# Windowed attention and a mixer block on one core: q and k tails transposed together, small scores moved, PSUM banks in turn

## The chip, the cores and the metric

The kernel runs on one core of a Trainium2 chip. The metric is the time of one execution on the device in microseconds (us). One execution was also recorded by the hardware profiler; times of single instructions come from that record. TensorE (PE, with its weight loads PEld) multiplies matrices into PSUM, which has eight banks here; VectorE (DVE) and ScalarE (ACT) read PSUM; GpSimd (POOL) works in SBUF; SyncE (SP) issues most DMAs. Each engine works through its own queue in order.

## What is computed

For each of 8 batches, attention over 8 heads with a window, and then a mixer block:

```python
scores = q @ k.T / 8                     # 8 batches, 8 heads, 576 positions, 64 wide
mask   = (0 <= i - j < 32)                           # heads 0 to 3
mask   = (0 <= i - j < 128) and (i - j) % 4 == 0     # heads 4 to 7
attn   = softmax(where(mask, scores, -1e9)) @ v
x      = attn with its heads side by side            # 8 x 576 x 512
u      = x + (relu(x.T @ w_tok1) @ w_tok2).T         # 576 -> 256 -> 576
out    = u + relu(u @ w_ch1) @ w_ch2                 # 512 -> 1536 -> 512
```

Inputs and outputs are fp32; the kernel computes in fp16 with fp32 sums in PSUM.

## The kernel before, in words

**Work of one batch.** POOL casts q, k and v to fp16 (names c_q, c_k, c_t, vv, vt). c_t holds the last 64 positions ("the tail") of q in its partitions 0 to 63 and of k in 64 to 127. For each pair of heads (hp 0 to 3; 0 and 1 have the plain window, 2 and 3 the dilated one), `transposes` (line 254) is called once for q and once for k. Each call makes four 128x128 transposes on TensorE (line 262) and a fifth of the tail (lines 266, 268), all into one bank, tp_q or tp_k. The tail transpose covers q's and k's tails together each time, and a permutation (`perm`) brings the wanted half to where it is read. The bank is then copied to SBUF: k by VectorE into kt (line 270), q into qz in two copies of 64 partitions, by ScalarE for pairs 0 and 1 (line 95) and by VectorE for pairs 2 and 3 (line 97).

The scores of a pair come in three steps (`scores_plain`, `scores_dil`, both with the product in line 284): the first scores of either head, each in one bank sc, and the "small scores" of both heads in a bank sm, which need the last keys. ScalarE takes the exponentials (lines 304, 313, 316 and 333, 341) and POOL multiplies them with the mask (line 107; batch 0 and part of batch 1 add the mask on TensorE, line 283). `values` multiplies with v into av, and VectorE divides (rec, xn). `emit_h1`, `emit_u` and `emit_uT` are the token mixer: h1p, up and tpu in PSUM, h1, u and uT in SBUF. `gen_main` is the channel mixer: 24 groups gp of four matmuls (line 496), each evicted by relu into gt (ACT line 101, DVE line 103), then groups yp (line 513; the two tails of an odd batch in line 533), summed with u into o (lines 523, 537) and stored.

**Order.** Batch 0 is prepared in an order written out by hand (calls `tp`, `sc`, `va`, `mx`). Then iteration b runs the channel mixer of batch b, and between its groups the steps of later batches: values and token mixer of batch b+1, transposes and scores of batch b+2 (iteration 0 does the scores of batches 1 and 2). `score_steps`, `value_steps` and `mix_steps` give each step a due time and a cost, and `interleave` calls a step when the sum of the costs so far reaches its due time. Nothing reorders afterwards: that is each engine's queue.

**PSUM.** `bank` (line 90) hands out banks under three tags: "fl" with three (tp_q, tp_k, av, h1p, up, tpu), "main" with three (gp, yp) and "sc" with two (sc, and sm from batch 1 on). Which of a tag's banks a tile gets is left to the pool. A matmul that starts a new tile in a bank waits until the copies out of the tile before have ended.

Of the kernel before, what the change touches and what calls it, by code (L numbers as in the profile page):

```python
# [16 lines left out]
S = 576  # L17
# [11 lines left out]
MR = S // 4  # L29

RS = 160
BLK = 160
# [6 lines left out]
GW = 2 * S  # L39


def _np_perm(first):

    m = np.zeros((128, 128), dtype=np.float16)
    for r in range(4):
        for i in range(32):
            half = (i // 16 + first) % 2
            m[64 * half + 4 * (i % 16) + r, 32 * r + i] = 1.0
    return m


def _np_band():
    p = np.arange(128)[:, None]
    rel = np.arange(BLK)[None, :] - p
    return ((rel >= 0) & (rel < WINDOW)).astype(np.float16)
# [14 lines left out]
def kernel(  # L70
# [11 lines left out]
    nc = tc.nc  # L82
# [4 lines left out]
    def fixed(name, shape, dtype=FP16):  # L87
        return sb.tile(shape, dtype, tag=name, bufs=1, name=name)

    def bank(tag, bufs, name, dtype=FP32):  # L90
        return ps.tile([128, 512 if dtype == FP32 else 1024], dtype, tag=tag, bufs=bufs, name=name)

    def copy(eng, out, in_):
        if eng is nc.scalar:
            nc.scalar.copy(out=out, in_=in_)  # L95
        else:
            eng.tensor_copy(out=out, in_=in_)  # L97
# [7 lines left out]
    def mult(eng, out, a, b):  # L105
# [1 line left out]
        eng.tensor_tensor(out=out, in0=x, in1=y, op=ALU.mult)  # L107


    CW = 3 * 128 + BLK + 128  # L110
    const = fixed("const", [128, CW])
    ident = const[:, 0:128]
    perm = [const[:, 128:256], const[:, 256:384]]
    band = const[:, 384:384 + BLK].rearrange("p (x y c) -> p x y c", x=1, y=1)
    dtail = const[:, 384 + BLK:CW].rearrange("p (x y c) -> p x y c", x=1, y=2)

    veil = fixed("veil", [128, BLK + 128])

    spread = fixed("spread", [128, 515])
    const_np = np.concatenate(  # L120
        [np.eye(128, dtype=np.float16), _np_perm(0), _np_perm(1), _np_band(),
         _np_dtail().reshape(128, 128)], axis=1)
    const_dram = nc.inline_tensor(const_np, name="consts").ap()

    qz = [fixed(f"qz{i}", [128, 2, S]) for i in range(4)]
    kt = [fixed(f"kt{i}", [128, 640]) for i in range(4)]
# [83 lines left out]
    c16 = {}  # L210
# [40 lines left out]
    def natural(ap):  # L251
        return ap.rearrange("p (m r) -> p m r", r=4)

    def transposes(b, nm, hp):
        c = c16[(b, nm)]
        p = bank("fl", 3, f"tp_{nm}_{b}_{hp}", FP16)
        tail = c16[(b, "t")][:, 2 * hp:2 * hp + 2, :].rearrange("m h d -> m (h d)")
        grid = p[:, 0:4 * RS].rearrange("p (r i) -> p r i", i=RS)
        got = grid[:, :, 0:MR].rearrange("p r m -> p m r")
        flat = nm == "q" and hp >= 2  # L260
        for r in range(4):
            nc.tensor.transpose(  # L262
                out=p[:, 128 * r:128 * r + 128] if flat else grid[:, r, 0:128],
                in_=c[:, r, 2 * hp:2 * hp + 2, :].rearrange("m h d -> m (h d)"), identity=ident)
        if flat:
            nc.tensor.transpose(out=p[:, 512:640], in_=tail, identity=ident)  # L266
        else:
            nc.tensor.transpose(out=grid[:, :, 128:RS], in_=tail, identity=perm[nm == "k"])  # L268
        if nm == "k":
            nc.vector.tensor_copy(out=natural(kt[hp][:, 0:S]), in_=got)  # L270
            return
        eng = nc.vector if hp >= 2 else nc.scalar
        for h in range(2):
            rows = slice(64 * h, 64 * h + 64)
            if flat:
                copy(eng, qz[hp][rows, h], p[rows, 0:S])
            else:
                copy(eng, natural(qz[hp][rows, h]), got[rows])

    def score(b, hp, h, out, keys, queries, hide):  # L280

# [144 lines left out]
    def emit_uT(b, cb):  # L426
        odd = b % 2
        c = slice(128 * cb, 128 * cb + 128)
        p = bank("fl", 3, f"tpu_{b}_{cb}", FP16)
        tl = u16t[b // 2][:, c]  # L430
        t = sb.tile([128, S], FP16, tag="ut", bufs=5, name=f"uT_{b}_{cb}")
        eng = nc.scalar if cb >= 2 else nc.vector
        if cb < 2:
            m0, t0, c0 = (128, 0, 64) if odd else (0, 512, 0)
            for s in range(4):
                nc.tensor.transpose(out=p[:, m0 + 128 * s:m0 + 128 * s + 128],
                                    in_=u16[(b, s)][:, c], identity=ident)
            nc.tensor.transpose(out=p[:, t0:t0 + 128], in_=tl, identity=ident)
            copy(eng, t, p[:, c0:c0 + S])
        else:  # L440
            grid = p[:, 0:4 * RS].rearrange("p (r i) -> p r i", i=RS)
            m0, t0, c0 = (32, 0, 16) if odd else (0, 128, 0)
            for s in range(4):
                nc.tensor.transpose(out=grid[:, s, m0:m0 + 128], in_=u16[(b, s)][:, c], identity=ident)  # L444
            nc.tensor.transpose(out=grid[:, :, t0:t0 + 32], in_=tl, identity=perm[0])  # L445
            copy(eng, natural(t), grid[:, :, c0:c0 + MR].rearrange("p r m -> p m r"))
        uT[(b, cb)] = t


    def score_steps(b, t0, dt):  # L450
        steps = []
        for hp in range(4):
            at = t0 + hp * dt
            for nm in ("q", "k"):
                steps.append((at + 0.9 * (nm == "k"), 0.28, lambda nm=nm, hp=hp: transposes(b, nm, hp)))
            g = (scores_plain if hp < 2 else scores_dil)(b, hp)
            for i in range(3):
                steps.append((at + dt + 0.6 * i, 0.21, lambda g=g: next(g)))
        return steps

    def value_steps(b, t0, dt):
# [6 lines left out]
            steps.append((t0 + dt * h, 0.29 if h < 4 else 0.18, step))  # L468
        return steps

    def mix_steps(b, t_h1, t_h1b, t_u, t_uT):
        if b % 2 == 0 and b // 2 not in u16t:
            u16t[b // 2] = sb.tile([128, DM], FP16, tag="u16t", bufs=2, name=f"u16t_{b // 2}")
        h1 = [sb.tile([128, DM], FP16, tag="h1", bufs=4, name=f"h1_{b}_{jb}") for jb in range(2)]
        steps = []
        for half, at in ((0, t_h1), (1, t_h1b)):
            for jb in range(2):
                steps.append((at + 0.9 * jb, 0.55, lambda jb=jb, half=half: emit_h1(b, jb, half, h1[jb])))
        for i, s in enumerate((4, 0, 1, 2, 3)):
            steps.append((t_u + 1.0 * i, 0.44, lambda s=s: emit_u(b, s, h1)))  # L480
        for i, cb in enumerate(CBS):
            steps.append((t_uT + 0.9 * i, 0.28, lambda cb=cb: emit_uT(b, cb)))
        return steps
# [99 lines left out]
    def gate(t, src):  # L583
# [1 line left out]

    cast_qk(0, "q", 0, nc.scalar)
    cast_qk(0, "k", 0, nc.vector)
    nc.vector.tensor_scalar(out=veil, in0=const[:, 384:CW], scalar1=1.0, scalar2=60000.0,
                            op0=ALU.subtract, op1=ALU.mult)
    cast_tails_qk(0, nc.vector)  # L590
    cast_qk(0, "q", 1, nc.gpsimd)
# [21 lines left out]
    for jb in range(2):  # L613
        nc.gpsimd.tensor_copy(
            out=w2p[jb], in_=w2[jb][:, 0:512].rearrange("p (m r) -> p r m", r=4))
# [56 lines left out]
    for i, n in enumerate(((0, 2), (2, 4), (4, 5))):  # L672
        nc.gpsimd.dma_start(
            out=w4a[:, 4 * i:4 * i + 4],
            in_=moe_w_ch2[512 * i:512 * i + 512, :].rearrange("(p i) c -> p i c", i=4))
# [13 lines left out]
    def at(t0, dt, fs):  # L689
        return [(t0 + dt * i, 0.0, f) for i, f in enumerate(fs)]  # L690
# [5 lines left out]
    for b in range(B):  # L696
        steps = []
        if b == 0:
            first, dil = score_steps(1, 5.5, 2.6), score_steps(1, 12.0, 2.0)
            steps += first[:10] + dil[10:]  # L700
            steps += at(14.4, 0.3, casts1_dil) + at(16.0, 0.5, casts1[9:])
            steps += at(15.7, 0.0, [lambda nm=nm: load_qk(2, nm, 4, 8, nc.sync) for nm in ("q", "k")])
            steps += at(23.0, 0.0, [lambda: load_v(2)])
            casts = cast_steps(2)
            steps += value_steps(1, 20.2, 0.7)
            steps += mix_steps(1, 23.0, 26.6, 28.2, 32.9) + score_steps(2, 25.4, 2.1)
            steps += at(21.7, 0.5, casts[:9]) + at(32.5, 0.3, casts[9:])
            steps += at(36.0, 0.0, [lambda: emit_loads_qk(3)])
        elif b == 1:
            steps += value_steps(2, 4.2, 1.0) + mix_steps(2, 10.0, 14.0, 16.6, 21.6)  # L710
            steps += score_steps(3, 21.0, 2.8) + at(8.0, 0.6, cast_steps(3))
            steps += at(6.0, 0.0, [lambda: load_v(3)]) + at(20.0, 3.0, [lambda: emit_loads_qk(4), lambda: load_v(4)])
        else:
            if b + 1 < B:
                steps += value_steps(b + 1, 0.6, 1.1) + mix_steps(b + 1, 6.6, 10.6, 13.2, 18.2)
            if b + 2 < B:
                steps += at(2.0, 0.6, cast_steps(b + 2)) + score_steps(b + 2, 20.6, 2.8)
            if b + 3 < B:
                steps += at(13.0, 3.0, [lambda b=b: emit_loads_qk(b + 3), lambda b=b: load_v(b + 3)])
        interleave(gen_main(b), steps)  # L720
# [30 lines left out]
```

## Time and profile before

| what | value |
|---|---|
| time, median of 3 runs | 320.54 us (320.04 to 321.05) |
| the profiled execution's own time | 320.02 us |
| its span, first to last instruction | 318.1 us |
| TensorE busy | 303.6 us, 3311 matmuls |
| VectorE, ScalarE, POOL busy | 166.2, 154.0, 152.9 us |
| granted TensorE clock | 1.0 throughout |
| DMA | 43.27 MB, mean 136 GB/s |
| the largest two groups, gp (line 496) and yp (line 513) | 109.4 and 91.9 us busy |

A row of the groups gives line, engine, operation, out<-in, shapes and count, then busy time in us and mean ns of one, then the engine's idle time ahead of them and what ended it. A row of the timeline gives the start in us from the span's start, the duration, the engine and line, and in brackets the idle time before it. Matmuls overlap, and their ends are modelled. The iterations of the channel mixer begin at about 31.1, 76.6, 114.5, 150, 187.5, 222.5, 260 and 289.6 us.

### The profile page before, as it was taken

Reading aid. Unit: us, or ns where it says so; the run is one execution under the profiler, and the core shown is the slowest. Engines: PE = TensorE matmul, PEld = TensorE weight load, DVE = VectorE, ACT = ScalarE, POOL = GpSimd, SP = SyncE. Lnnn points to the kernel's source line nnn. Section 1 sums busy time; section 2 is a strip of 40 time slices with the busy share of each in tenths; the row PEclk is TensorE's granted clock in tenths of the full one; section 3 lists DMA queues with packets and bytes.
Section 4 is the critical chain, followed back from the end, with each engine's and each line's share of the span. In section 5 each row is a group of like instructions: output and inputs, shape, how many; then the busy total and the mean of one; then the engine's idle time right before and its main releaser. Section 6 shows DMA issues by size and latency. Waiting matters only on the chain.

```text
span 318.1 us, 8187 instructions
## 1 busy us (share of the span) xinstructions
PE 303.6 (95%) x3311; PEld 269.2 (85%) x3311; DVE 166.2 (52%) x356; ACT 154.0 (48%) x349; POOL 152.9 (48%) x218
## 2 busy tenths in 40 slices
PE   6888999989999999999999999999999999999995
PEld 2676888869978889899987999899987999899884
DVE  6564536773736545555745636545745636532221
ACT  2674594385445535365554635465454725413500
POOL 8771466569840896019930797009940670000000
PEclk9999999999999999999999999999999999999999
DMA  8999999823945979711593139811000220012022
GB/s 214 276 195 244 193 243 277 242 77 84 339 110 154 273 226 285 158 43 58 149 290 89 40 107 297 163 36 68 33 2 5 63 101 3 0 48 86 2 68 99
DMA packets 66597, 43.27 MB, mean 136 GB/s; under 512 B 35936, under 2 KB 64992, under 8 KB 66560
## 3 DMA queue, kind: packets, MB, share of 16 engines
q1 hardware_dynamic: 63328, 37.63, 43.2%
q0 software_dynamic: 1632, 3.94, 6.7%
q10 hardware_dynamic: 1600, 1.18, 1.4%
q8 instruction: 26, 0.43, 0.6%
q14 instruction: 11, 0.09, 0.1%
HBM read 37.07 MB, written 9.44 MB: 146 GB/s over the span
## 4 chain that ended last, share of the span: by engine, by line
PE 87%; DVE 5%; ACT 5%; issue 1%; POOL 0%; ACTq 0%; POOLq 0%
PE gp L496 29%; PE yp L513 25%; PE up L407 4%; PE h1p L395 4%; PE sc L284 4%; PE yp L533 3%; PE tp_q L262 2%; PE sm L284 2%; PE idle_p L561 2%; ACT qz L95 2%; PE tp_k L262 1%; PE h1p L393 1%; DVE kt L270 1%; PE tpu L444 1%; PE av L371 1%
## 5 line engine op out<-in xcount | busy, mean ns | idle before, releaser
L496 PE MATMUL gp<-uT,w 128*128 128x288 f16 x768 | 109.4, 286 | 0.5 <-ACT gt L101 0.3
L101 ACT ACTIVATE gt<-gp 128x288 f16<-128x288 f32 x138 | 56.5, 411 | 76.2 <-PE gp L496 68.2
L513 PE MATMUL yp<-w,gt 128*128 128x256 f16 x756 | 91.9, 273 | 0.0
L496 PEld LDWEIGHTS <-w 128*128 128x128 f16 x768 | 83.2, 113 | 7.8 <-issue 1.0
L107 POOL TENSOR_TENSOR attp<-attp,const 128x1280 f16<-128x1280 f16 (+1 forms) x28 | 41.7, 1521 | 85.5 <-ACT attp L313 74.4
L513 PEld LDWEIGHTS <-gt 128*128 128x128 f16 x768 | 76.6, 106 | 4.1
L103 DVE TENSOR_SCALAR gt<-gp 128x288 f16<-128x288 f32 x54 | 24.6, 455 | 35.6 <-PE gp L496 33.6
L523 DVE TENSOR_TENSOR o<-yp,u 128x512 f32<-128x512 f32 x31 | 21.4, 691 | 40.2 <-PE yp L513 37.5
L284 PEld LDWEIGHTS <-kt 128*128 128x128 f16 x352 | 26.9, 103 | 7.2 <-issue 3.1
L107 POOL TENSOR_TENSOR attd<-attd,const 128x1024 f16<-128x1024 f16 (+1 forms) x24 | 32.9, 1401 | 0.0
L107 DVE TENSOR_TENSOR xn<-av,rec 128x320 f16<-128x320 f32 x62 | 30.5, 492 | 2.1
L270 DVE COPY kt<-tp_k 128x576 f16<-128x576 f16 x32 | 24.2, 755 | 10.3 <-PE tp_k L268 9.8
L333 ACT ACTIVATE attd<-sc 128x512 f16<-128x512 f32 x32 | 17.9, 595 | 22.0 <-PE sc L284 20.6
L95 ACT COPY qz<-tp_q 64x576 f16<-64x576 f16 x32 | 20.2, 630 | 11.5 <-PE tp_q L268 11.1
L284 PE MATMUL sc<-qz,kt 128*128 128x128 f16 (+1 forms) x224 | 24.5, 226 | 1.2 <-DVE kt L270 0.6
L414 DVE TENSOR_TENSOR u<-up,xn 128x512 f16<-128x512 f32 x28 | 19.3, 691 | 6.8 <-PE up L407 6.7
L304 ACT ACTIVATE attp<-sc 128x480 f16<-128x480 f32 x32 | 17.6, 577 | 8.6 <-PE sc L284 8.4
L97 DVE COPY qz<-tp_q 64x576 f16<-64x576 f16 x32 | 14.5, 454 | 11.3 <-PE tp_q L266 11.1
L97 POOL CAST c_q<-l_q 128x512 f16<-128x512 f32 x29 | 17.9, 619 | 3.2 <-DMA l_q<-in_q_dram 3.2
L379 DVE RECIPROCAL rec<-av 128x5 f32<-128x5 f32 x64 | 12.2, 192 | 12.8 <-PE av L366 7.2
L97 POOL CAST c_k<-l_k 128x512 f16<-128x512 f32 x27 | 16.7, 618 | 3.3 <-DMA l_k<-in_k_dram 3.3
L95 ACT COPY uT<-tpu 128x576 f16<-128x576 f16 x16 | 10.1, 638 | 13.3 <-PE tpu L445 13.3
(114 smaller groups left out, 449.8 us busy)
## 6 DMA issues: line engine op xcount, KB each, us to landing
out_dram<-o SPq DMA_DIRECT2D x72, 128.0 KB, 2.0
l_q<-in_q_dram SPq DMA_DIRECT2D x15, 512.0 KB, 5.8
l_k<-in_k_dram SPq DMA_DIRECT2D x14, 512.0 KB, 6.8
l_vn<-in_v_dram SPq DMA_DIRECT2D x32, 128.0 KB, 6.2
l_vd<-in_v_dram SPq DMA_DIRECT2D x16, 256.0 KB, 4.8
w<-in_moe_w_ch_dram POOLq DMA_DIRECT2D x4, 384.0 KB, 6.3
w<-in_moe_w_ch_dram POOLq DMA_DIRECT2D x3, 512.0 KB, 6.1
lt<-in_q_dram SPq DMA_DIRECT2D x8, 128.0 KB, 3.5
```

What stands on the lines that cost most here:

```text
L95: nc.scalar.copy(out=out, in_=in_)
L97: eng.tensor_copy(out=out, in_=in_)
L101: nc.scalar.activation(out=out, in_=in_, func=AF.Relu)
L103: eng.tensor_scalar_max(out=out, in0=in_, scalar1=0.0)
L107: eng.tensor_tensor(out=out, in0=x, in1=y, op=ALU.mult)
L270: nc.vector.tensor_copy(out=natural(kt[hp][:, 0:S]), in_=got)
L284: nc.tensor.matmul(out=out, lhsT=kt[hp][:, keys], rhs=qz[hp][:, h, queries], start=hide is None, stop=True)
L333: nc.scalar.activation(out=a[:, h, 0:DTL], in_=p, func=AF.Exp, scale=0.125)
L414: nc.vector.tensor_tensor(out=t, in0=p, in1=xn[b][:, s], op=ALU.add)
L496: nc.tensor.matmul(out=p[:, 0:288], lhsT=w3[cb][:, 512 * (mb // 4) + mb % 4:512 * (mb // 4) + 512:4], rhs=uT[(b, cb)][:, 288 * sh:288 * sh ...
L513: nc.tensor.matmul(out=p[:, c], lhsT=gt[(b // 2, mb)][:, a0:m0 + 512:4] if half else gt[(b // 2, mb)][:, a0:a0 + 128], rhs=w4[mb][:, c], s ...
L523: nc.vector.tensor_tensor(out=o32, in0=p, in1=u16[(b, s)], op=ALU.add)
```

## The change

The k call of `transposes` makes no tail transpose any more and copies 512 columns. The q call's tail transpose serves both: behind the q copies, VectorE copies k's 64 columns out of the same bank tp_q into kt (lines 287 and 289 of the new file). One permutation matrix is left. `bank` counts tiles of "main" and "sc" and gives each of their banks a tag of its own, so that they are used strictly in turn. The three score steps of a pair are due 0.0, 0.7 and 2.0 behind their base instead of 0.0, 0.6 and 1.2, with other offsets in iteration 0; the scores of batch 3 begin 0.8 later; and in iteration 0 the token mixer's steps and the scores of batch 2 are due later and wider apart.

```diff
+    turn = {"main": 0, "sc": 0}
     def bank(tag, bufs, name, dtype=FP32):
+        if tag in turn:
+            turn[tag] += 1
+            tag, bufs = f"{tag}{turn[tag] % bufs}", 1
         return ps.tile([128, 512 if dtype == FP32 else 1024], dtype, tag=tag, bufs=bufs, name=name)
...
     def transposes(b, nm, hp):
         c = c16[(b, nm)]
         p = bank("fl", 3, f"tp_{nm}_{b}_{hp}", FP16)
-        tail = c16[(b, "t")][:, 2 * hp:2 * hp + 2, :].rearrange("m h d -> m (h d)")
         grid = p[:, 0:4 * RS].rearrange("p (r i) -> p r i", i=RS)
-        got = grid[:, :, 0:MR].rearrange("p r m -> p m r")
-        flat = nm == "q" and hp >= 2
+        flat = nm == "k" or hp >= 2
         for r in range(4):
             nc.tensor.transpose(
                 out=p[:, 128 * r:128 * r + 128] if flat else grid[:, r, 0:128],
                 in_=c[:, r, 2 * hp:2 * hp + 2, :].rearrange("m h d -> m (h d)"), identity=ident)
+        if nm == "k":
+            nc.vector.tensor_copy(out=natural(kt[hp][:, 0:512]),
+                                  in_=p[:, 0:512].rearrange("p (r m) -> p m r", r=4))
+            return
+        tail = c16[(b, "t")][:, 2 * hp:2 * hp + 2, :].rearrange("m h d -> m (h d)")
         if flat:
             nc.tensor.transpose(out=p[:, 512:640], in_=tail, identity=ident)
         else:
-            nc.tensor.transpose(out=grid[:, :, 128:RS], in_=tail, identity=perm[nm == "k"])
-        if nm == "k":
-            nc.vector.tensor_copy(out=natural(kt[hp][:, 0:S]), in_=got)
-            return
+            nc.tensor.transpose(out=grid[:, :, 128:RS], in_=tail, identity=perm)
         eng = nc.vector if hp >= 2 else nc.scalar
         for h in range(2):
             rows = slice(64 * h, 64 * h + 64)
             if flat:
                 copy(eng, qz[hp][rows, h], p[rows, 0:S])
             else:
-                copy(eng, natural(qz[hp][rows, h]), got[rows])
+                copy(eng, natural(qz[hp][rows, h]), grid[rows, :, 0:MR].rearrange("p r m -> p m r"))
+        if flat:
+            nc.vector.tensor_copy(out=kt[hp][:, 512:S], in_=p[:, S:640])
+        else:
+            nc.vector.tensor_copy(out=natural(kt[hp][:, 512:S]),
+                                  in_=grid[:, :, MR:RS].rearrange("p r m -> p m r"))
...
-    def score_steps(b, t0, dt):
+    def score_steps(b, t0, dt, offs=(0.0, 0.7, 2.0)):
...
-                steps.append((at + dt + 0.6 * i, 0.21, lambda g=g: next(g)))
+                steps.append((at + dt + offs[i], 0.21, lambda g=g: next(g)))
...
-    def mix_steps(b, t_h1, t_h1b, t_u, t_uT):
+    def mix_steps(b, t_h1, t_h1b, t_u, t_uT, du=1.0):
...
-            steps.append((t_u + 1.0 * i, 0.44, lambda s=s: emit_u(b, s, h1)))
+            steps.append((t_u + du * i, 0.44, lambda s=s: emit_u(b, s, h1)))
...
         if b == 0:
-            first, dil = score_steps(1, 5.5, 2.6), score_steps(1, 12.0, 2.0)
+            first, dil = score_steps(1, 5.5, 2.6, (0.0, 0.6, 1.8)), score_steps(1, 12.0, 2.0, (0.0, 0.6, 1.2))
...
-            steps += mix_steps(1, 23.0, 26.6, 28.2, 32.9) + score_steps(2, 25.4, 2.1)
+            steps += mix_steps(1, 23.8, 27.2, 28.9, 34.2, 1.2) + score_steps(2, 25.4, 2.4, (0.0, 0.6, 1.6))
...
         elif b == 1:
...
-            steps += score_steps(3, 21.0, 2.8) + at(8.0, 0.6, cast_steps(3))
+            steps += score_steps(3, 21.8, 2.8) + at(8.0, 0.6, cast_steps(3))
```

More of the change, by code (lines that the diff above doesn't have):

```diff
@@ L39, with _np_perm @@
 GW = 2 * S
-def _np_perm(first):
+def _np_perm():
     m = np.zeros((128, 128), dtype=np.float16)
@@ L46, in _np_perm @@
         for i in range(32):
-            half = (i // 16 + first) % 2
+            half = i // 16
             m[64 * half + 4 * (i % 16) + r, 32 * r + i] = 1.0
@@ L107, in mult @@
         eng.tensor_tensor(out=out, in0=x, in1=y, op=ALU.mult)
-    CW = 3 * 128 + BLK + 128
+    CW = 2 * 128 + BLK + 128
     const = fixed("const", [128, CW])
     ident = const[:, 0:128]
-    perm = [const[:, 128:256], const[:, 256:384]]
-    band = const[:, 384:384 + BLK].rearrange("p (x y c) -> p x y c", x=1, y=1)
-    dtail = const[:, 384 + BLK:CW].rearrange("p (x y c) -> p x y c", x=1, y=2)
+    perm = const[:, 128:256]
+    band = const[:, 256:256 + BLK].rearrange("p (x y c) -> p x y c", x=1, y=1)
+    dtail = const[:, 256 + BLK:CW].rearrange("p (x y c) -> p x y c", x=1, y=2)
     veil = fixed("veil", [128, BLK + 128])
@@ L120 @@
     const_np = np.concatenate(
-        [np.eye(128, dtype=np.float16), _np_perm(0), _np_perm(1), _np_band(),
+        [np.eye(128, dtype=np.float16), _np_perm(), _np_band(),
          _np_dtail().reshape(128, 128)], axis=1)
@@ L444, in emit_uT @@
                 nc.tensor.transpose(out=grid[:, s, m0:m0 + 128], in_=u16[(b, s)][:, c], identity=ident)
-            nc.tensor.transpose(out=grid[:, :, t0:t0 + 32], in_=tl, identity=perm[0])
+            nc.tensor.transpose(out=grid[:, :, t0:t0 + 32], in_=tl, identity=perm)
             copy(eng, natural(t), grid[:, :, c0:c0 + MR].rearrange("p r m -> p m r"))
         uT[(b, cb)] = t
-    def score_steps(b, t0, dt):
+    def score_steps(b, t0, dt, offs=(0.0, 0.7, 2.0)):
         steps = []
@@ L587 @@
     cast_qk(0, "k", 0, nc.vector)
-    nc.vector.tensor_scalar(out=veil, in0=const[:, 384:CW], scalar1=1.0, scalar2=60000.0,
+    nc.vector.tensor_scalar(out=veil, in0=const[:, 256:CW], scalar1=1.0, scalar2=60000.0,
                             op0=ALU.subtract, op1=ALU.mult)
```

## The prediction

> **What bounds the kernel now.** I read the page first (busy shares, chain), then the list of waits, then the timeline around each wait of TensorE.
>
> ```profile
> PE 303.6 (95%) x3311; PEld 269.2 (85%) x3311; DVE 166.2 (52%) x356; ACT 154.0 (48%) x349; POOL 152.9 (48%) x218
> ...
> PE 87%; DVE 5%; ACT 5%; issue 1%; POOL 0%; ACTq 0%; POOLq 0%
> ```
>
> TensorE is the bound, and the chain that ended last runs through it for 87% of the span. So the time moves by TensorE's work and by its stalls. A busy record is no measure of either, because matmuls overlap; I use the distance from one matmul's start to the next. Undisturbed it is 123 ns for 288 columns, 109 for 256, 69 for 160, 56 for 128 and 29 for 64. Summed over all matmuls that is 293.7 us; what a distance has on top is a stall. By stage the stalls are 7.7 us up to 31.1 us (start and batch 0), 1.1 to 46.2, 0.65 to 57.1, 3.7 to 76.6 (these three are iteration 0), then 1.2, 1.3, 0.7, 0.9, 0.7 for iterations 1 to 5 (to 114.5, 150, 187.5, 222.5, 260), and 0.15 behind that.
>
> A steady iteration's stalls look like this (timeline of iteration 2, the scores of batch 4):
>
> ```profile
> 136.50 1.29 ACT L95 COPY qz<-tp_q 64x576 f16<-64x576 f16 x2
> 136.59 0.46 DVE L97 COPY uT<-tpu 128x576 f16<-128x576 f16 x1 [1.03 <-ACT uT L95]
> ...
> 137.18 0.69 DVE L523 TENSOR_TENSOR o<-yp,u 128x512 f32<-128x512 f32 x1
> ...
> 137.79 0.75 DVE L270 COPY kt<-tp_k 128x576 f16<-128x576 f16 x1
> ...
> 138.59 0.38 PE L284 MATMUL sc<-qz,kt 128*128 128x160 f16 x3
> ...
> 139.07 0.57 ACT L304 ACTIVATE attp<-sc 128x480 f16<-128x480 f32 x1 [1.28 <-PE sc L284]
> ...
> 139.52 0.22 PE L268 MATMUL tp_k<-const,c_t 128*128 128x128 f16 x1
> 139.52 0.40 PEld L284 LDWEIGHTS <-kt 128*128 128x128 f16 x4
> 139.54 1.28 ACT L95 COPY qz<-tp_q 64x576 f16<-64x576 f16 x2
> 139.69 0.36 PE L284 MATMUL sm<-qz,kt 128*128 128x160 f16 x4
> ```
>
> From 139.52 to 139.69 is 0.17 us instead of 0.056: the small scores (sm) take the bank of the first scores and wait 0.115 us for their exponential, which ends at 139.64. Pair 1 does the same, and pair 2 waits 0.405 us (145.40 to 145.86, behind a 128x512 exponential). That is 0.64 us in each of iterations 2 to 5. Note also that kt is ready at 138.54 and its scores start at 138.59: nothing is spare there.
>
> **The change, part by part.**
>
> *Small scores later.* In the built program's order 1.3 us of yp matmuls now stand between tp_k and sm in pairs 0 and 2, and 0.65 us in pair 1. The exponentials end before that, so the 0.64 us go. What is late next: the first scores of pair 1, now 3.07 us behind those of pair 0, need the bank whose exponential ended 2.82 us behind them (141.41), so this holds by 0.2 us. The mask products on POOL come about 1 us later; POOL waited 74.4 us for these inputs, the four pairs take it 11.7 us, and the first values that need them stand in the next iteration, so they cost nothing; without that room it would be that 1 us once per batch.
>
> *Banks in turn.* The order of the main and sc banks differs only in iterations 0 and 2. There one bank was used twice running: gp at 116.40 waited 0.435 us for ACT's gt. This goes, once.
>
> *One tail transpose per pair.* 32 transposes fewer. Price: 56 ns from start to start, 32 x 0.056 = 1.8 us, 0.22 us per batch; the first batch's four lie in waits.
>
> ```profile
> L270 DVE COPY kt<-tp_k 128x576 f16<-128x576 f16 x32 | 24.2, 755 | 10.3 <-PE tp_k L268 9.8
> ...
> L268 PE MATMUL tp_k<-const,c_t 128*128 128x128 f16 x32 | 7.0, 219 | 0.0
> ```
>
> The second row gives 219 ns each, but the matmul behind starts 56 ns later where nothing else is awaited, so I take 56; were it 219, the gain would be 7.0 us (a rival below). The Trainium skill (TensorE: Matmul & The Clock Gate, "Part 4: PE-mode transpose") gives about 275 ns for a 128x128 transpose within a kernel. By that the gain would be 32 x 0.275 = 8.8 us; the trace's 56 ns speak against it.
>
> *The new copy.* VectorE's kt copy shrinks from 576 to 512 columns, and 32 copies of 128x64 out of tp_q's bank are added. VectorE's rows out of PSUM grow from 492 ns (320 columns) to 691 (512), 1.04 ns per column on a fixed 160. So kt takes 690, and the new copy 0.22 us; the bounds are 192 (the reciprocal of 128x5) and 455 ns (128x288). It is small, but its place matters. For pairs 0 and 1 the queries are copied from that same bank by ACT, and in the built program the new copy waits for the second of these ACT copies. Behind it, in VectorE's queue, stand a uT copy, an o sum and the kt copy that the scores need. No row of before shows a tile read by both engines, so the price is the queue's sum:
>
> - Iterations 2 and 4, pair 0: ACT ends at 137.79. New copy 137.84, uT 137.99, o 138.37, kt 138.98 to 139.67 (starts by the rows' distances, 0.15, 0.38, 0.61). The scores are there at 138.53: stall 1.15 us. Iterations 3 and 5, by the same sum from 172.40: 0.97. If the wait cost nothing this would be 0; if the copy took 455 ns, 0.25 more.
> - Pair 1: ACT ends 2.23 us behind pair 0's first scores, kt is ready at 3.11, its scores come at 3.07: 0.1 us.
> - Pairs 2 and 3 copy q on VectorE itself: kt comes 0.1 us later, and had 0.5 to spare in the steady state.
>
> The Trainium skill (PSUM — Partial Sum Buffer, "PSUM bank collisions raise a hardware error") says that two engines may not access one bank in the same 32 partitions at once, two reads included. By it this wait is no accident of the build, and the sum without it (316.0, a rival) is out of reach. No run here shows the collision.
>
> Sum: iteration 2: 1.25 - 0.64 - 0.435 - 0.22 = 0.0; iteration 4: +0.4; 3 and 5: 1.07 - 0.86 = +0.2 each. **Together +0.8.**
>
> *The start* is where the wait falls on a bare chain:
>
> ```profile
> 8.51 2.59 ACT L95 COPY qz<-tp_q 64x576 f16<-64x576 f16 x4 [3.31 <-PE tp_q L268]
> ...
> 8.79 0.76 DVE L270 COPY kt<-tp_k 128x576 f16<-128x576 f16 x1 [1.47 <-PE tp_k L268]
> ...
> 9.47 0.51 DVE L97 CAST c_k<-l_k 128x512 f16<-128x512 f32 x1
> ...
> 10.03 0.40 PE L262 MATMUL tp_k<-const,c_k 128*128 128x128 f16 x4 [0.41 <-DVE c_k L97]
> ```
>
> ACT's second copy ends at 9.80, so kt runs 10.0 to 10.68 and the cast behind it 10.6 to 11.12; tp_k of pair 1 starts at 11.17 instead of 10.03. The first scores follow at 11.39, their exponential at 12.0 instead of 11.13: 0.87 us, and ACT is gapless from there to 14.1. Two more new copies on VectorE before pair 3's scores make it **+1.0**. Nothing up to 31 us waits for a load, so I take none of it back.
>
> *Iteration 0 and 1.* I repeated this queue sum from group to group. 31 to 46: sm's waits (0.89) go, pair 1's kt costs 0.57 and two transposes pairs 0.1 less: **-0.4**. 46 to 57: kt of pairs 2 and 3 is awaited there already, behind VectorE's q copies: **+0.15**. 57 to 76: the wider steps take away 0.59 (scores for kt at 67.9), 0.39 (71.8) and 0.35 (h1 and values at 57 to 59); new are 1.1 at up_1_4, whose bank is now that of tp_q (ACT ends about 64.9), and 0.25 at pair 0's scores; and the last u sum now stands behind two more copies on VectorE right ahead of its transpose, which waits 1.2 to 1.8 us instead of 0.79. With four transposes fewer: **0.0**, give or take 1. Iteration 1: scores 0.8 later now mix with uT: 1.15 of stalls go, 1.6 come (tp_k for uT's bank 0.35, tpu for tp_q's bank 0.6, pair 1's kt 0.45, two small ones), less 0.22: **+0.25**. The loads' issues keep their places between the same gp and yp groups.
>
> Total: 1.0 - 0.4 + 0.15 + 0.0 + 0.25 + 0.8 = **+1.8 us**. The profiled execution took 320.02 us (span 318.1), so 321.8; it lay 0.5 below the median of 320.54, and on that I forecast 322.3.
>
> **Rivals.**
>
> 1. *The wait costs nothing* (ACT copies earlier, or the copies overlap): then the terms above without it are +0.3, -0.4, +0.15, -0.3, -0.4 and, for iterations 2 to 5, -1.3 and three times -0.86: -4.5, 316.0 us. This is the other side; it turns where ACT's second q copy ends 1.2 us before kt must start. Against it: 137.79 is exactly when kt started. Chance 0.08.
> 2. *The start is absorbed*: the DMA engines are full up to 57 us (share 1.0), so a later start could meet loads that would have been waited for. That takes the 1.0 back: 321.3, within the noise. Against it: no TensorE stall there ends at a load. Chance 0.20.
> 3. *Iteration 0 tangles*: the stalls at up_1_4 and at the u transpose (1.1 and 1.2 to 1.8) come on top of those that I took as gone: +2, 324.3. For it: these rest on the longest sum. Chance 0.12.
> 4. *The transposes cost their record*, 7.0 instead of 1.8: 317.1. Chance 0.02.
> 5. *The small scores still wait* (ACT is later than they are moved): +3, 325.3. Chance 0.03.
>
> **How the numbers follow.** The forecast has 0.55, with a range of its own of 321.2 to 323.6 (0.1 us on the new copy is 0.1 in each of ten places). A measurement of this kernel tells about 0.3%, 0.96 us: 319.6 to 321.5 is no change. Faster: rivals 1 and 4 and 0.04 of the forecast's edge, 0.14. Same: rival 2 and 0.04, 0.24. Slower: the rest, 0.62. The range 319.9 to 324.4 leaves rivals 1 and 4 below and 5 above.
>
> **What would show it.** Right: in the waits, DVE kt (line 289) for ACT qz about 1 us each, sixteen times; PE sc for DVE kt about 1 us once per steady iteration; no PE sm for ACT; the second tp_k at about 11.2 us. Wrong: kt (line 270) at its old distance from tp_k, or iterations 2 to 5 shorter than 145 us together (they are 145.5 now, from 114.5 to 260).

## The result, and the profile after

The changed kernel took 322.21 us (median of 12 runs, 321.33 to 323.58), the kernel before 320.66 (12 runs, 319.81 to 321.2). The ratio is 1.005, with a 95% interval of 1.0036 to 1.0065: slower by 1.55 us, where +1.8 was forecast. The profiled execution of the changed kernel took 322.81 us with a span of 320.3; before's took 320.02 with 318.1. The two profiles thus lie 2.2 us apart in span, 0.6 more than the medians; the start has this difference (below).

The same two rows of the page as those shown of before, busy time and chain:

```profile
PE 300.6 (94%) x3279; PEld 266.1 (83%) x3279; DVE 167.0 (52%) x388; ACT 154.6 (48%) x349; POOL 152.5 (48%) x218
...
PE 80%; DVE 8%; ACT 6%; POOL 2%; issue 2%; DMA 1%; SPq 0%; ACTq 0%; POOLq 0%; DVEq 0%
```

TensorE has 32 matmuls fewer and VectorE 32 copies more, as the diff says. But TensorE's part of the chain fell from 87% to 80%, and VectorE's rose from 5% to 8%: work was taken off the engine that sets the time, and waiting was put in its place. The two rows of the groups with the price of the copies, kt (682 ns, forecast 690) and the new tail copy of pairs 0 and 1 (224 ns, forecast 0.22 us; the last figure is idle time ahead of them):

```profile
L270 DVE COPY kt<-tp_k 128x512 f16<-128x512 f16 x32 | 21.8, 682 | 0.9 <-PE tp_k L266 0.9
...
L289 DVE COPY kt<-tp_q 128x64 f16<-128x64 f16 x16 | 3.6, 224 | 30.2 <-ACT qz L101 30.2
```

The list of waits (engine and tile that waits, what it waits for, us in total, times, longest), first one row of before and then three of after:

```profile
PE sc L284 <- DVE kt L270: 0.6, 2, 0.4
...
DVE kt L289 <- ACT qz L101: 30.2, 15, 2.5
...
PE sc L296 <- DVE kt L270: 4.1, 7, 1.0
...
DVE o L535 <- DMA out_dram<-o: 3.1, 1, 3.1
```

The first row of after (line 289) is the predicted wait, the second what it does to TensorE (4.1 us in seven waits, 0.6 us in two before). The third was not foreseen. No wait of sm for ScalarE is left (before: 1.7 us in six). The timeline of iteration 2, at the place shown of before, tells the mechanism:

```profile
137.93 1.29 ACT L101 COPY qz<-tp_q 64x576 f16<-64x576 f16 x2
...
139.26 0.23 DVE L289 COPY kt<-tp_q 128x64 f16<-128x64 f16 x1 [2.33 <-ACT qz L101]
139.40 0.45 DVE L103 COPY uT<-tpu 128x576 f16<-128x576 f16 x1
139.76 0.68 DVE L535 TENSOR_TENSOR o<-yp,u 128x512 f32<-128x512 f32 x1
140.36 0.68 DVE L270 COPY kt<-tp_k 128x512 f16<-128x512 f16 x1
...
141.10 0.38 PE L296 MATMUL sc<-qz,kt 128*128 128x160 f16 x3 [0.99 <-DVE kt L270]
```

Read it from the end. The scores start at 141.10, where kt ends at 141.04. kt starts when o lets it, o behind uT, uT behind the small copy, and that starts at 139.26, 0.04 us after ScalarE's second q copy ended at 139.22. VectorE stood idle for 2.33 us, with three other jobs queued behind the small one. From start to start of matmuls the stall is 1.153 us (forecast 1.15); iterations 3, 4 and 5 have 0.942, 1.151 and 0.944 (forecast 0.97, 1.15, 0.97).

A clean measure of each part is the distance from the first gp matmul of an iteration to that of the next, in the timeline of TensorE. In kernels that differ in another place only it repeats within 0.03 us, so the tables below use it. (These starts lie up to 0.7 us ahead of the rounded ones in the prediction.)

| us | start | it. 0 | it. 1 | it. 2 | it. 3 | it. 4 | it. 5 | it. 6 | it. 7 to the last matmul |
|---|---|---|---|---|---|---|---|---|---|
| before | 30.39 | 46.08 | 37.93 | 35.45 | 37.44 | 35.02 | 37.44 | 29.72 | 24.99 |
| after | 32.13 | 45.53 | 38.11 | 35.81 | 37.53 | 35.28 | 37.54 | 29.70 | 24.99 |
| difference | +1.74 | -0.55 | +0.18 | +0.36 | +0.09 | +0.26 | +0.10 | -0.02 | 0.00 |
| forecast | +1.0 | -0.25 | +0.25 | 0.0 | +0.2 | +0.4 | +0.2 | 0 | 0 |

### The profile page after: what moved, and what is told of

It is laid out like the page before. It is cut to its first block, busy times and chain, and to the rows that moved or that the text cites. A ratio compares the mean times of both kernels' runs of the same rounds, so it can differ in the third digit from the quotient of the medians.

```text
span 320.3 us, 8148 instructions
## 1 busy us (share of the span) xinstructions
PE 300.6 (94%) x3279; PEld 266.1 (83%) x3279; DVE 167.0 (52%) x388; ACT 154.6 (48%) x349; POOL 152.5 (48%) x218
## 4 chain that ended last, share of the span: by engine, by line
PE 80%; DVE 8%; ACT 6%; POOL 2%; issue 2%; DMA 1%; SPq 0%; ACTq 0%; POOLq 0%; DVEq 0%
PE gp L508 28%; PE yp L525 19%; ACT qz L101 4%; PE sc L296 4%; PE up L419 4%; PE h1p L407 4%; PE yp L545 3%; DVE kt L270 2%; PE idle_p L573 2%; PE tp_q L266 2%; POOL attp L113 1%; DVE qz L103 1%; PE tpu L456 1%; PE sm L296 1%; PE up L432 1%
## 5 line engine op out<-in xcount | busy, mean ns | idle before, releaser
L525 PE MATMUL yp<-w,gt 128*128 128x256 f16 x756 | 94.0, 273 | 0.0
L270 DVE COPY kt<-tp_k 128x512 f16<-128x512 f16 x32 | 21.8, 682 | 0.9 <-PE tp_k L266 0.9
L289 DVE COPY kt<-tp_q 128x64 f16<-128x64 f16 x16 | 3.6, 224 | 30.2 <-ACT qz L101 30.2
```

The lines of the kernel that those rows point to most:

```text
L270: nc.vector.tensor_copy(out=natural(kt[hp][:, 0:512]), in_=p[:, 0:512].rearrange("p (r m) -> p m r", r=4))
L525: nc.tensor.matmul(out=p[:, c], lhsT=gt[(b // 2, mb)][:, a0:m0 + 512:4] if half else gt[(b // 2, mb)][:, a0:a0 + 128], rhs=w4[mb][:, c], s ...
```

## The experiments

The theory: VectorE's tail copy of pairs 0 and 1 must wait for ScalarE's q copies out of the same bank, and what stands behind it in VectorE's queue, kt above all, reaches TensorE late; this eats what the later small scores and the 32 saved transposes bring. The rivals: the transposes' own cost (219 ns each by their record), the price of the small copy, the moved steps. The runs of a group shared the runs of before, whose median is 320.54 us for tails_only to act_tail, 321.09 for offs_only to late_loads, and 320.89 for the last three, so kernels of different groups are compared by their ratios.

| kernel | ratio to before, 95% | start | it. 0 | it. 1 | it. 2 to 5 |
|---|---|---|---|---|---|
| before | 1 | 30.39 | 46.08 | 37.93 | 145.35 |
| after | 1.0050 (1.0036 to 1.0065) | 32.13 | 45.53 | 38.11 | 146.16 |
| tails_only | 1.0194 (1.0178 to 1.0209) | 32.29 | 47.08 | 38.77 | 148.73 |
| no_tails | 0.9874 (0.9852 to 0.9896) | 30.52 | 44.06 | 37.37 | 143.45 |
| late_tail | 0.9841 (0.9820 to 0.9861) | 30.90 | 44.11 | 37.27 | 142.21 |
| act_tail | 0.9859 (0.9845 to 0.9874) | 31.60 | 44.45 | 37.39 | 142.44 |
| offs_only | 0.9896 (0.9877 to 0.9915) | 31.20 | 46.11 | 37.65 | 142.68 |
| turn_only | 0.9998 (0.9984 to 1.0012) | 30.84 | 46.11 | 37.93 | 145.88 |
| late_old_spread | 0.9910 (0.9893 to 0.9928) | 31.88 | 46.50 | 38.27 | 141.91 |
| late_loads | 0.9770 (0.9751 to 0.9788) | 30.59 | 44.11 | 37.28 | 141.27 |
| after_old_spread | 1.0086 (1.0063 to 1.0110) | 32.19 | 47.08 | 38.51 | 146.29 |
| after_loads | 1.0039 (1.0019 to 1.0059) | 33.88 | 45.54 | 38.12 | 145.63 |
| late_all_loads | 0.9792 (0.9776 to 0.9808) | 31.43 | 44.45 | 37.19 | 141.28 |

### The shared tail transposes: alone, left out, and with the copy elsewhere

**tails_only**: before, with the changed `transposes` and nothing else.

```diff
-        flat = nm == "q" and hp >= 2
+        flat = nm == "k" or hp >= 2
...
-            nc.tensor.transpose(out=grid[:, :, 128:RS], in_=tail, identity=perm[nm == "k"])
-        if nm == "k":
-            nc.vector.tensor_copy(out=natural(kt[hp][:, 0:S]), in_=got)
...
+            nc.vector.tensor_copy(out=natural(kt[hp][:, 512:S]),
+                                  in_=grid[:, :, MR:RS].rearrange("p r m -> p m r"))
```

> The kernel before with the transposes of after and nothing else of the change. Theory (the copy of k's tail waits in VectorE's queue for ScalarE's q copies and holds up kt): slower than before by more than the whole change, since the small scores' waits (0.64 us in each of iterations 2 to 5) are not taken away: start +1.2, iterations 2 to 5 +0.7 to +0.9 each, iterations 0 and 1 +1 to +2, in all +5, 324.5 to 327 us beside 320.6. Rival (the wait is hidden, the 32 transposes saved count): 1.8 us faster, about 319.

326.82 us (before 320.54): this part alone costs 6.3 us, and every section of the table is longer. Pair 0's scores wait 1.152, 0.946, 1.153 and 0.944 us for kt in iterations 2 to 5, the same numbers as in the changed kernel. One row of its waits answers the question about the saved transposes:

```profile
PE sm L290 <- ACT attd L339: 1.5, 5, 0.3
```

Before, the same wait (for the 128x512 exponential) was shorter:

```profile
PE sm L284 <- ACT attd L333: 1.2, 5, 0.2
```

A transpose of 56 ns was taken away ahead of sm, and sm's stall grew from 0.405 to 0.462 us: a matmul saved ahead of a wait that has another end is only waited out. In pairs 0 and 1 the same stall grew from 0.115 to 0.172 us. So of the four transposes saved in an iteration, three pay nothing until the small scores are moved; only pair 3 has no such wait.

**no_tails**: the changed kernel with before's `transposes` and its two permutations.

```diff
-        flat = nm == "k" or hp >= 2
+        flat = nm == "q" and hp >= 2
...
+            nc.tensor.transpose(out=grid[:, :, 128:RS], in_=tail, identity=perm[nm == "k"])
+        if nm == "k":
+            nc.vector.tensor_copy(out=natural(kt[hp][:, 0:S]), in_=got)
```

> After without the common tail transpose (transposes and copies as before; banks in turn, moved scores and spread stay). Theory: what is left are gains: the small scores' waits go (4 x 0.64), the bank wait of iteration 2 (0.44), 0.3 to 0.9 in iterations 0 and 1: 316.3 to 317.7 us, and no stall of the scores for kt of pair 0 in iterations 2 to 5. Rival (the moved scores and the spread are what cost): as slow as after or slower, 322 us or more.

316.38 us. Without the shared transposes the rest of the change is faster than before by 4.2 us. Iterations 2 to 5 take 143.45 us with them left out and 146.16 with them, and no stall of pair 0's scores for kt is left there. One part of the theory failed: the bank wait of iteration 2 did not go. There gp waits 1.198 us for an o sum, so that this iteration takes 35.54 us, 0.09 more than before (see turn_only).

**late_tail**: the changed kernel; the tail copies of pairs 0 and 1 are issued behind the same pair's kt copy, so that nothing that is needed soon stands behind the wait.

```diff
+    held = {}
...
             nc.vector.tensor_copy(out=natural(kt[hp][:, 0:512]),
                                   in_=p[:, 0:512].rearrange("p (r m) -> p m r", r=4))
+            if hp < 2:
+                nc.vector.tensor_copy(out=natural(kt[hp][:, 512:S]),
+                                      in_=held.pop(hp)[:, :, MR:RS].rearrange("p r m -> p m r"))
             return
...
-            nc.vector.tensor_copy(out=natural(kt[hp][:, 512:S]),
-                                  in_=grid[:, :, MR:RS].rearrange("p r m -> p m r"))
+            held[hp] = grid
```

> After, with the 128x64 copy of k's tail for pairs 0 and 1 moved from behind the q copies to behind the kt copy of the same pair: same work, same bank rule, but kt no longer stands behind the wait. Theory: pair 0's stall (1.15 and 0.95 us in iterations 2 to 5) goes, the start loses about 0.3 instead of 1.2: about 4 us faster than before, 316 to 317.5 us. Rival (the 128x64 copies themselves or the flat k layout cost): no change against after, 322 us.

315.72 us, a little better than expected. Same copies, same transposes, another place in one queue: 6.5 us from the changed kernel's 322.21 (6.7 by the ratios). In its timeline of iteration 2, kt starts right behind the o sum ahead of it, the tail copy follows without a wait, and the scores have no stall:

```profile
136.14 0.68 DVE L272 COPY kt<-tp_k 128x512 f16<-128x512 f16 x1
...
136.74 0.21 DVE L275 COPY kt<-tp_q 128x64 f16<-128x64 f16 x1
...
136.88 0.38 PE L300 MATMUL sc<-qz,kt 128*128 128x160 f16 x3
```

Over the whole kernel the wait for ScalarE's q copies falls from 30.2 us to

```profile
DVE kt L275 <- ACT qz L101: 3.0, 7, 0.4
```

This run also gives the transposes' price. In iterations 3 to 5 late_tail and no_tails have the same few stalls, 0.2 us at most, and they differ by 0.23, 0.26 and 0.23 us (36.55 for 36.78, 34.09 for 34.35, 36.55 for 36.78). Four transposes of 56 ns are 0.22. The Trainium skill ("TensorE: Matmul & The Clock Gate", "Part 4: PE-mode transpose") gives about 275 ns for one; by that, as an estimate, 1.1 us would lie between them. The measurement decides: back to back, a 128x128 transpose of fp16 takes 56 ns of TensorE's time here.

**act_tail**: the changed kernel, with these tail copies on ScalarE, behind its own q copies.

```diff
-            nc.vector.tensor_copy(out=natural(kt[hp][:, 512:S]),
+            nc.scalar.copy(out=natural(kt[hp][:, 512:S]),
                                   in_=grid[:, :, MR:RS].rearrange("p r m -> p m r"))
```

> After, with the copy of k's tail of pairs 0 and 1 given to ScalarE, right behind its two q copies: no engine waits for another there. Theory: kt is on time again, and ScalarE has 0.25 us more per pair, which costs 0.5 at the start and 0.1 to 0.3 where the next exponential follows: 316 to 318 us. Rival (ScalarE is what holds the first scores, not VectorE's queue): as after or slower, 322 us or more.

316.13 us. With only one engine reading the bank there is no wait between engines, and the stalls go too. ScalarE's 16 copies more cost 0.4 us against late_tail by the medians; by the profiles they cost 0.34 us in iteration 0, 0.12 in iteration 1 and 0.23 in iterations 2 to 5. So neither the transposes nor the copy is what costs, but the wait in VectorE's queue and what is queued behind it.

### The other parts, one at a time

**offs_only**: before, with the small scores' offsets of iterations 1 and later.

```diff
-    def score_steps(b, t0, dt):
+    def score_steps(b, t0, dt, offs=(0.0, 0.7, 2.0)):
...
-                steps.append((at + dt + 0.6 * i, 0.21, lambda g=g: next(g)))
+                steps.append((at + dt + offs[i], 0.21, lambda g=g: next(g)))
```

> The kernel before, with the small scores 0.7 and 2.0 behind the first ones (0.6 and 1.2 before) in the iterations from the second on, and nothing else of the change. Theory (the waits of the small scores for ScalarE's exp are real stalls of TensorE and this part of the change alone takes them away): 0.64 us in each of iterations 2 to 5, and up to 0.5 in iteration 1, so 317.3 to 318.2 us beside 320.5. Rival (a wait that is spread over instructions only moves, and comes back as a wait of sc for a bank or for kt): 319.8 to 320.8.

317.7 us (before 321.09). Iterations 2 to 5 shrink by 2.67 us, or 0.67 each where the stalls of sm were 0.64, and iteration 1 by 0.28. In iterations 2 to 5 the waits went and did not come back elsewhere; in iteration 1 new stalls of sc (0.37 and 0.14 us, where before had one of 0.26) took a part back.

**turn_only**: before, with `bank` counting the tiles of "main" and "sc", as in the diff of the change.

> The kernel before, with the PSUM banks of the tags main and sc taken strictly in turn, and nothing else. Theory (it takes away one wait of gp for ScalarE's copy of gt, 0.435 us in iteration 2, or leaves it as a wait for the next thing): 320.0 to 320.6 us. Rival (turns cost something, since a bank that is free earlier is passed over): 321 us or more.

321.01 us (before 321.09), ratio 0.9998: no difference in time. By its number this lies in the rival's range, but the before known when it was set was 320.54; by the ratio, which gives 320.5 beside that, it lies in the theory's. Yet the trace shows what the rival says, a bank passed over that would have been free earlier: the stall which was to go became a longer one. Before, gp waited 0.435 us for ScalarE's gt at the start of iteration 2; now the next bank in turn is one that a yp sum still holds, and gp waits 0.979 us for it. The first row is of before, the second of turn_only:

```profile
116.86 0.78 PE L496 MATMUL gp<-uT,w 128*128 128x288 f16 x5 [0.27 <-ACT gt L101]
...
117.12 0.65 PE L501 MATMUL gp<-uT,w 128*128 128x288 f16 x4 [0.82 <-DVE o L528]
```

That o sum itself starts only at 116.37, 0.12 us behind the landing of the output transfer that held its SBUF buffer. In before, too, VectorE stood idle for 2.42 us until this sum started 0.12 us behind such a landing, but no gp needed its bank: the turn made a harmless wait into one of TensorE. Iteration 2 takes 35.98 instead of 35.45 us. That loss of 0.53 us is not in the times, whose interval ends at +0.4 us; whether all executions have it is open.

**after_old_spread** and **late_old_spread**: the changed kernel and late_tail, each with before's step times in iterations 0 and 1.

```diff
-            first, dil = score_steps(1, 5.5, 2.6, (0.0, 0.6, 1.8)), score_steps(1, 12.0, 2.0, (0.0, 0.6, 1.2))
+            first, dil = score_steps(1, 5.5, 2.6, (0.0, 0.6, 1.2)), score_steps(1, 12.0, 2.0, (0.0, 0.6, 1.2))
...
-            steps += mix_steps(1, 23.8, 27.2, 28.9, 34.2, 1.2) + score_steps(2, 25.4, 2.4, (0.0, 0.6, 1.6))
+            steps += mix_steps(1, 23.0, 26.6, 28.2, 32.9) + score_steps(2, 25.4, 2.1, (0.0, 0.6, 1.2))
...
-            steps += score_steps(3, 21.8, 2.8) + at(8.0, 0.6, cast_steps(3))
+            steps += score_steps(3, 21.0, 2.8) + at(8.0, 0.6, cast_steps(3))
```

> The version with the tail copy behind the same pair's kt copy, but with the step times of the first two iterations as in the kernel before. Theory (the spread steps are worth little once the wait in DVE's queue is gone): between 315.5 and 317.2 us, beside 315.7 with the spread steps. Rival (the spread steps are the part that carries the gain in iteration 0, where before lost 3.7 us of stalls between 57 and 77 us): over 317.5.

318.29 us: my theory for this run was wrong. Iteration 0 takes 46.50 us without the spread steps and 44.11 with them, iteration 1 38.27 and 37.27 (iteration 2 is 0.30 shorter without them). So the spread steps carry 3.1 us by the profiles, and 2.2 by the ratios, in a kernel that does not wait for the tail copy.

> The changed kernel with the step times of the first two iterations as before. Theory (the spread steps are worth about as much beside the shared transposes as they were beside the later tail copy, where they brought some 2.2 us): 323.8 to 324.8 us beside 322.2 with them. Rival (beside the shared transposes the spread steps gain nothing, as the prediction's terms of +0.15 and 0.0 for the stretch from 46 to 76 us had it, and only 0.4 us ahead of that): 322.3 to 323.0.

323.66 us, just under the expected range, and outside the rival's. In the changed kernel the spread steps are worth 1.55 us in iteration 0 (47.08 to 45.53) and 0.40 in iteration 1. By the ratios the difference is 1.2 us, and the two intervals just overlap, so the size rests on the iteration lengths.

### The wait that was not foreseen

In the changed kernel, too, gp waits for o at the start of iteration 2, by 0.518 us. These rows of its timeline are of SP's queue (SPq), VectorE and TensorE:

```profile
112.97 4.88 SPq L541 DMA_DIRECT2D out_dram<-o  x7
113.01 0.69 DVE L535 TENSOR_TENSOR o<-yp,u 128x512 f32<-128x512 f32 x1 [1.16 <-PE yp L525]
...
116.80 0.69 DVE L535 TENSOR_TENSOR o<-yp,u 128x512 f32<-128x512 f32 x1 [3.10 <-DMA out_dram<-o]
...
117.54 0.28 PE L508 MATMUL gp<-uT,w 128*128 128x288 f16 x1 [0.36 <-DVE o L535]
```

VectorE stands idle for 3.10 us ahead of the second o, because its SBUF buffer (one of three) still holds an earlier result: SP issues those output transfers only from 112.97 on, because the loads of batch 4's v fill its queue from 102.9 to 112.9.

**late_loads** and **after_loads**: late_tail and the changed kernel, each with the loads of batch 4 issued earlier (POOL's casts of batch 3, which free the buffers, end at 88.8 us).

```diff
-            steps += at(6.0, 0.0, [lambda: load_v(3)]) + at(20.0, 3.0, [lambda: emit_loads_qk(4), lambda: load_v(4)])
+            steps += at(6.0, 0.0, [lambda: load_v(3)]) + at(13.0, 3.0, [lambda: emit_loads_qk(4), lambda: load_v(4)])
```

> The version with the tail copy behind the same pair's kt copy, and the loads of batch 4 issued 7 us earlier in the second iteration (13.0 and 16.0 in place of 20.0 and 23.0; batch 3's casts, which free the buffers, end at 88.8 us). Theory (the wait of gp for DVE's o, which waits for the output transfers that SP issues only behind the loads of v, is caused by the place of these loads): the stall of 0.94 us at 113.5 goes, 314.6 to 315.0 us beside 315.7. Rival (the output transfers are late for a reason of their own, or gp then waits for the next thing): 315.5 to 316.

313.71 us (before 321.09 in this group), below the expected range. The output transfers are issued from 100.6 us on, the stall is gone, and iteration 2 takes 34.09 us, exactly as long as iteration 4 (late_tail: 35.02).

```profile
100.60 13.10 SPq L545 DMA_DIRECT2D out_dram<-o  x8
```

The trace gives 0.93 us to this; the ratio fell by more, from 0.9841 to 0.9770 (2.3 us), and nothing in the profiles explains the rest. The two come from different groups of runs.

> The changed kernel with the loads of batch 4 issued 7 us earlier in the second iteration, and nothing else. Theory (the one wait that the prediction did not foresee, gp for DVE's o behind the output transfers, 0.52 us at 117.0, comes from the place of these loads): it goes, 321.4 to 321.9 us beside 322.2. Rival (the wait for ScalarE's copy of gt that stood there in the kernel before, 0.44 us, is under it and comes back, or the loads disturb another stage): 322.1 or more.

Iteration 2 shrinks from 35.81 to 35.28 us and the wait is gone, as the theory had it. The time, 322.17 us (ratio 1.0039, interval 1.0019 to 1.0059), can't be told from the changed kernel's (1.0036 to 1.0065): by its number it lies at the edge of the rival's range, and the runs spread from 320.87 to 323.69. The rival's own mechanism did not come: no wait for gt stands there. That iteration 0 of the profiled execution starts only at 33.88 us has another reason: the granted TensorE clock was 0.50 for 3.4 us from 12.3 us on (1.00 around it), and from the second tp_k to the first gp passed 21.72 us instead of the changed kernel's 20.14. So the cause is shown in the trace, the half microsecond in the time is not.

**late_all_loads**: late_loads, with the tail copies of pairs 2 and 3 behind kt too.

```diff
-            if hp < 2:
+            if hp >= 2:
+                nc.vector.tensor_copy(out=kt[hp][:, 512:S], in_=held.pop(hp)[:, S:640])
+            else:
                 nc.vector.tensor_copy(out=natural(kt[hp][:, 512:S]),
...
-        if flat:
-            nc.vector.tensor_copy(out=kt[hp][:, 512:S], in_=p[:, S:640])
-        else:
-            held[hp] = grid
+        held[hp] = p if flat else grid
```

> The fastest version so far (tail copy behind the same pair's kt copy for pairs 0 and 1, loads of batch 4 earlier) with the tail copy behind kt for pairs 2 and 3 as well. Theory (kt of these pairs comes 0.2 us earlier, but no sc waits for it in the steady iterations any more): 313.3 to 313.9 us beside 313.7. Rival (in the first iterations, where sc does wait for kt, each such wait gets 0.2 us shorter): 312.6 to 313.2.

314.27 us, missed by both: the steady iterations are unchanged, and iteration 0 is 0.34 us longer (up waits there 0.839 us for VectorE's kt copies, 0.324 in late_loads). late_loads is the fastest of these kernels, 2.3% faster than before (ratio 0.9770, interval 0.9751 to 0.9788).

## Why the prediction was right, step by step

- **Small scores later**: 0.64 us forecast in each of iterations 2 to 5, 0.67 measured (offs_only). Right.
- **The tail copy in VectorE's queue**: pair 0's four stalls came out within 0.03 us of the queue sums. Their first condition, that the copy waits for ScalarE's second copy, is shown by the rows and by late_tail, which removes the harm by place alone. The prediction expected the copy's wait at about 1 us each; VectorE's idle time is 2.0 each (30.2 in 15, where sixteen were expected). This made no difference, because what counts is when the wait ends, not how long the engine has stood.
- **32 transposes, 1.8 us**: 56 ns each is confirmed (late_tail against no_tails). The rival of 219 ns each is out. But tails_only shows that they count only where no other wait ends behind them.
- **Banks in turn, -0.435 us**: wrong. I named the wait that goes and not what is late next. gp got the bank of a yp sum in its place, whose o waited for output transfers: 0.979 us in turn_only and 0.518 in the changed kernel, so +0.54 and +0.08. This is why iteration 2 came out at +0.36 instead of 0.0. Iterations 2 to 5 are +0.81 in sum, where +0.8 was forecast: this error cancelled, by luck, against terms in the other three that were some 0.1 us too high each (pair 1's scores were to lose 0.1 us; in iteration 2 it is 0.046).
- **The start, +1.0**: the mechanism is right, the size in this profile (+1.74) is not. The first row is of before, the rest of the changed kernel:

```profile
2.53 5.67 PE L561 MATMUL idle_p<-idle 128*128 128x512 f16 x18 [2.53 <-POOL idle L144]
...
2.53 6.16 PE L573 MATMUL idle_p<-idle 128*128 128x512 f16 x18 [2.53 <-POOL idle L150]
...
9.01 2.59 ACT L101 COPY qz<-tp_q 64x576 f16<-64x576 f16 x4 [3.54 <-PE tp_q L278]
...
10.33 0.23 DVE L289 COPY kt<-tp_q 128x64 f16<-128x64 f16 x1 [2.43 <-ACT qz L101]
10.47 0.68 DVE L270 COPY kt<-tp_k 128x512 f16<-128x512 f16 x1
...
11.07 0.86 DVE L103 CAST c_k<-l_k 128x512 f16<-128x512 f32 x1
...
11.99 0.40 PE L266 MATMUL tp_k<-const,c_k 128*128 128x128 f16 x4 [2.30 <-DVE c_k L103]
```

  The second tp_k was forecast at 11.17 and came at 11.99. The first tp_q came 0.50 us later than before (8.53 for 8.03). That is not the new copy's doing: TensorE first runs 18 matmuls on an idle tile (idle_p), which start 0.43 us apart at first and 0.22 later, and in this execution the step came later, so that they took 6.16 us instead of 5.67. The tail, cast by 7.9, was not awaited. Then the c_k cast took 0.86 us instead of 0.51. From first tp_q to second tp_k are 2.00 us before, 3.46 here, and 3.01 in tails_only and in after_old_spread, where that cast takes 0.42: about 1.0 for the wait (forecast 1.14), 0.45 for the cast. From the second tp_k to the first gp the changed kernel takes 0.22 us less (20.14 for 20.36). So +1.74 is 0.50 + 1.46 - 0.22; the part that tails_only and after_old_spread show too is the wait less the 0.22, 0.8 us. In after_loads the stretch from tp_q to tp_k is 4.29 us, because c_t's load came late (TensorE waits 1.10 us for it). The iterations behind the start add up to +0.42, so the medians' +1.55 leave some 1.1 to the start.

  One reading of the prediction was wrong, without harm here: it says that nothing up to 31 us waits for a load, but in before POOL's c_q cast waits 0.60 us for its load until 8.51, and the second tp_q stalls 0.371 us for that cast.
- **Iteration 0, -0.25 in sum; measured -0.55.** It is a difference of two larger things: the shared transposes cost 1.00 us there (tails_only against before), and the spread steps bring 1.55. The foreseen single stalls came: 1.057 us at up_1_4 (forecast 1.1), 1.017 at the u transpose (a little under the 1.2 to 1.8 forecast), 0.378 at pair 0's scores (0.25). Two of 0.32 and 0.30 us behind the tail copies of pairs 2 and 3 were not foreseen.
- **Iteration 1, +0.25; measured +0.18**, with tp_k for uT's bank 0.331 (0.35), tpu for tp_q's bank 0.572 (0.6) and pair 1's scores 0.421 (0.45).
- **Rivals.** The wait that costs nothing (316.0 us) is no property of the change as it stands, but late_tail reaches 315.72 by placing the copy elsewhere. The prediction called that sum out of reach by a rule of the Trainium skill (PSUM — Partial Sum Buffer, "PSUM bank collisions raise a hardware error"). The rule forbids only that both engines access the bank at once, and no run shows them doing so; what I drew from it was too much, since the wait may stand where nobody needs the queue. Small scores that still wait and a tangled iteration 0 did not come, and the medians leave no sign of an absorbed start.

## What to carry to other kernels

When an instruction gets a new wait, write down what stands behind it in its engine's queue and when each of these is needed: here 16 copies of 0.22 us turned a change worth 4 to 5 us into a loss of 1.6, and moving them behind one other copy gave it all back. Work saved ahead of a wait that ends elsewhere only lengthens the wait, so remove the wait first, then count. Before a resource wait is booked as a gain, ask which holder comes next, and look as far as the DMA queue that frees its buffer.

## What was not expected of the hardware

Iteration lengths of different kernels repeat within 0.03 us wherever their code agrees (36.55, 36.55, 36.54 and 36.55 us for iteration 3 of four of them), while the first gp came between 30.39 and 31.20 us in the four profiles with before's transposes: what scatters most in the profiles is the start. Three things are seen to move it. The step of the idle matmuls from 0.43 to 0.22 us came anywhere from the seventh to the fourteenth of them, so that the first tp_q started anywhere from 7.87 to 9.31 us. Loads came late (c_t's in after_loads). And in that profile alone the granted clock fell to 0.50 for 3.4 us. Why the step and the clock come when they do, no run here shows.

The c_k cast of pair 1 (128x512, fp32 to fp16, on VectorE) took 0.42 to 0.53 us in twelve of the thirteen profiles, but 0.86 in the changed kernel's, where a cast of POOL began 0.03 us ahead of it. In after_old_spread, with POOL's cast 0.02 us ahead, it took 0.42 while POOL's pair of casts took 1.45 us instead of 1.16. Overlapping work of these two engines is thus lengthened on one side or the other; what decides which is open. The Trainium skill (Advanced Engine Details and Errata, "Mode Summary") says that VectorE's second SBUF port is shared with GpSimd, so that GpSimd's instructions and those of VectorE that use both ports interfere with or block each other. The longer casts agree with that in kind; whether these casts use the second port, no run here shows.
